# Retention attention and a squared-ReLU FFN on one core: attention visits of two chunks, another seven-product scheme, fixed rows of operations

## The chip, the cores and the metric

The kernel runs on one core of one Trainium2 chip. The metric is the device time of one execution in microseconds; the time shown is the median of several runs. The profiles are those of one execution each, and their span reaches from the first to the last instruction.

TensorE (PE in the profile) multiplies, VectorE (DVE), ScalarE (ACT) and GpSimd (POOL) do the elementwise work, and SyncE (SP) issues nearly all transfers. Each engine executes its own instructions in the order in which they were emitted and waits on semaphores for the others.

## The reference

```python
state = np.zeros((B, H, D, D), dtype=np.float32)
for t in range(S):
    state = gamma[None, :, None, None] * state + np.einsum('bhd,bhe->bhde', k[:, :, t], v[:, :, t])
    y[:, :, t] = scale * np.einsum('bhd,bhde->bhe', q[:, :, t], state)
...
x = np.ascontiguousarray(attn_out.transpose(0, 2, 1, 3)).reshape(B * S, H * D)
h = np.maximum(x @ w_in, 0.0)
return (h * h @ w_out).astype(np.float32)
```

There are 4 batches of 768 positions, 8 heads of 64; this gives 3072 tokens of 512 numbers. w_in is 512 x 2048, w_out 2048 x 512. All inputs and the output are float32; the kernel multiplies in bf16.

## The kernel before, in words

**Attention by chunks.** The tokens are cut into 24 chunks of 128 (six for each batch), each of two halves of 64. For a chunk, the kernel forms scores of keys against queries inside each half, masks them (P, into `pt`), and forms the sum of key times value of each half. These sums are added up to the running states (S, `state`). The output is values times masked scores plus the state applied to the queries (`apply`, first within the half's own row group, then `cross` after a drain of TensorE and a semaphore), scaled and written to `xt` by Y. The chunks 0 to 3 go in pairs in another layout (`together`, `pair_visits`). From chunk 4 on, `visit(m, n)` is one stretch on TensorE: values and states of chunk m, with scores and sums of chunk n between its two applies. The scores lie in one half of each bank of `sc`, the sums in the other; `yy` holds the outputs. All of these are 64 x 64 matmuls. The keys and queries must first be cast to bf16 (ck, cq) and transposed to `qkT`: on TensorE for the first chunks, from chunk 7 on by a DMA transpose on SP (X, line 761).

**FFN.** The chunks are grouped in 13 blocks of one or two. `ffn1` (F1) multiplies w_in by a block's `xt` in groups, one PSUM bank of 512 numbers each: eight matmuls of 128 x 256 for a block of two chunks, sixteen of 128 x 128 for a block of one. A bank is read by R (ReLU on ScalarE, into one of two buffers `r`) and squared into `h` by Q (ScalarE or VectorE). For the first four chunks `ffn2` (F2) multiplies plainly by w_out. For the others `products` does two chunks (a unit, named by its first chunk) by a scheme of seven products instead of eight: the 2 x 2 blocks are two chunks by two halves of the 2048 inner columns on one side, two halves of the inner rows by two halves of the output columns on the other. Five sums of blocks of `h` per unit (S1, S2, S5, S6, S7, line 1007), five sums of blocks of w_out (T1, T3, T4, T6, T7, in two halves each, made once, line 982), seven products M1 to M7 of eight matmuls each (line 1032), and reads that combine them: e4 and cc on ScalarE (128 x 256 and 128 x 512), t1, u1, w, c on VectorE (two of 128 x 256, two of 128 x 512; line 1050).

**Banks.** Four PSUM banks `fps` are shared by the F1 groups, F2, the products (a unit holds two, A and B, from their first product to the last read), and the transposes of the first chunks.

**The order.** All operations are recorded in a `Plan` with durations, dependencies and priorities. `schedule` places them one by one, each time the one that could start first by its model, ties by priority. Two tables steer it: `HOME` fixes the engine of some operations, `RANK` the priority of others. `dma_order` ranks the loads. The operations are then emitted in the order of their planned starts, and that order is what each engine executes. Around the first 65 us the loads of q, k, v and of the two weights (1 MB or 512 KB each) come through SP's queue in that order; each weight piece is cast to bf16 (cwin, cwout) on POOL, ScalarE or VectorE before it is used.

Of the kernel before, what the change touches and what calls it, by code (L numbers as in the profile page):

```python
# [18 lines left out]
class Plan:  # L19
# [14 lines left out]
    HOP = 0.15  # L34

# [5 lines left out]
    def add(self, name, eng, dur, reads=(), writes=(), fn=None, prio=0.0, lat=0.0, bank=None, after=(), count=0, slot=None, lock=()):  # L41
# [19 lines left out]
        if name in HOME:  # L61
            eng = {HOME[name]: eng[HOME[name]]}
        prio = RANK.get(name, prio)
        self.ops.append(dict(i=i, name=name, eng=eng, flex=flex, deps=sorted(deps), fn=fn,
                             prio=prio, lat=lat, bank=bank, count=count, slot=slot, lock=lock))
        return i

    def schedule(self, nbanks, max_open, nslots):
# [12 lines left out]
        for o in ops:  # L81
            for e in o["eng"]:
                eng_free.setdefault(e, 0.0)
                pool.setdefault(e, set())
                if left[o["i"]] == 0:
                    pool[e].add(o["i"])
# [15 lines left out]
        while done < n:  # L102
            best = None
            for eng, cand in pool.items():
                ef = eng_free[eng]
                for i in cand:
# [17 lines left out]
                    key = (t, o["prio"], i)  # L124
                    if best is None or key < best[0]:
                        best = (key, i, eng)
            assert best is not None, "no operation can be placed"
            (t, _, _), i, eng = best
            o = ops[i]
            for e in o["eng"]:  # L130
                pool[e].discard(i)
# [34 lines left out]
            else:  # L166
                if eng == "PE":
# [21 lines left out]
                    if any(before < x <= issued for x in range(self.BLOCK0 - self.AHEAD, issued + 1, self.BLOCK)):  # L189
# [14 lines left out]
                end[i] = t + dur + o["lat"]  # L204
# [15 lines left out]
            for u in users[i]:  # L220
                same = list(ops[u]["eng"]) == [eng] and not move
                ready_at[u] = max(ready_at[u], start[i] + dur if same else end[i] + self.HOP)
                left[u] -= 1
                if left[u] == 0:
                    for e in ops[u]["eng"]:
                        pool[e].add(u)
# [11 lines left out]
AHEAD = 4  # L238
WARM = 20.0
FILL = 0.215  # L240
WARMING = 18.4
PACE = 8
LEAD = 2
# [5 lines left out]
CVT = {'DVE': 0.69, 'POOL': 1.07}  # L249
TCAST = {'DVE': 0.43, 'ACT': 0.63, 'POOL': 0.64}  # L250
TEVAC = {'ACT': 0.6, 'DVE': 0.62}
NPAIR = 2
F2LAG = 3.5
F2WAIT = 4
LAST = [256, 128, 128]
CAST = {"k": {"DVE": 0.43, "ACT": 0.63, "POOL": 0.64}, "q": {"DVE": 0.43, "ACT": 0.63, "POOL": 0.64}}
WCAST = {"DVE": 0.43, "ACT": 0.63, "POOL": 0.64}
EVAC = {"ACT": 0.6, "DVE": 0.62}
WPRIO = {"in": -2.0, "out": 2.0, "sum": 3.0}
# [3 lines left out]
SQUARE = {"DVE": 0.7, "ACT": 0.63}  # L263
WSUM = {"DVE": 0.69}
ASUM = {"DVE": 0.69}
LAGS = {
# [941 lines left out]
```

## Time and profile before

| | |
|---|---|
| time, median of 3 runs | 203.87 us (203.72 to 205.05) |
| span of the profiled execution | 202.7 us (its own time is not listed; the median is 1.2 us longer than this span) |
| granted TensorE clock | 1.000 |
| busy: TensorE, its weight loads, VectorE, ScalarE, GpSimd | 192.8, 159.4, 150.0, 130.3, 31.3 us |
| F1 groups (L936): 832 matmuls | 94.0 us |
| products (L1032): 560 matmuls | 70.1 us (39.4 + 20.3 + 10.4) |
| plain F2 (L1108): 64 matmuls | 15.0 us |
| transfers | 38.46 MB, mean 190 GB/s |

How to read it: a matmul's time runs from its start to its modelled end, and matmuls overlap, so a mean of 264 ns for one does not mean that one comes every 264 ns; the steps in the chain do (eight in 0.87 us). The elementwise engines overlap too: neighbours on VectorE start 0.60 us apart where each is shown with 0.68. "Idle before" with an arrow names what ended the wait.

### The profile page before, as it was taken

The numbers are of one execution on the slowest core, as the hardware profiler recorded it, in microseconds if no ns is written. First come the engines' busy times: TensorE is split into PE (matmuls) and PEld (weight loads), VectorE is DVE, ScalarE is ACT, GpSimd is POOL, SyncE is SP. The second block draws the span as 40 slices with busy tenths as digits, with TensorE's granted clock in tenths as the row PEclk, the third lists the DMA queues.
The fourth block names the chain that finished last, engine by engine and source line by source line (L and its number), as shares of the span: only waits on it lengthen the run. The fifth ranks groups of instructions, "written<-read, shape, count | busy, mean of one in ns | idle before, by whom it ended". The sixth has DMA issues, their size and how long they took to land.

```text
span 202.7 us, 7020 instructions
## 1 busy us (share of the span) xinstructions
PE 192.8 (95%) x3032; PEld 159.4 (79%) x3032; DVE 150.0 (74%) x283; ACT 130.3 (64%) x229; POOL 31.3 (15%) x56
## 2 busy tenths in 40 slices
PE   8886999899989999999999999999999999999992
PEld 6554887664577888888888888888888888888881
DVE  3486449569849988969898888878998784934762
ACT  8565888788871883787975485569375873835210
POOL 6541252220102101310211012203010000000000
PEclk9999999999999999999999999999999999999999
DMA  5999999999999999999999999999676100111313
GB/s 159 290 314 320 348 344 330 361 246 210 236 191 219 231 247 212 205 234 186 148 240 165 261 211 218 178 222 194 143 145 97 48 17 3 52 52 55 102 55 105
DMA packets 97935, 38.46 MB, mean 190 GB/s; under 512 B 81008, under 2 KB 94320, under 8 KB 97904
## 3 DMA queue, kind: packets, MB, share of 16 engines
q1 hardware_dynamic: 97760, 37.89, 86.2%
q8 instruction: 23, 0.38, 0.8%
q10 hardware_dynamic: 144, 0.13, 0.2%
q14 instruction: 8, 0.07, 0.1%
HBM read 27.26 MB, written 6.29 MB: 166 GB/s over the span
## 4 chain that ended last, share of the span: by engine, by line
PE 75%; DMA 15%; SPq 5%; POOL 1%; DVE 1%; issue 1%; ACT 0%; DVEq 0%
PE fps L936 33%; PE fps L1032 29%; DMA kn<-in_k_dram 8%; PE fps L1108 6%; DMA wst<-in_moe_w_in_dram 4%; DMA qkT<-kqs 3%; SPq L910 3%; PE yy L787 2%; SPq L537 2%; PE yy L802 1%; PE sc L813 1%; PE sc L824 1%; POOL w_in L522 1%; DVE wu L1050 1%; POOL h L522 0%
## 5 line engine op out<-in xcount | busy, mean ns | idle before, releaser
L936 PE MATMUL fps<-xt,w_in 128*128 128x256 bf16 (+1 forms) x832 | 94.0, 264 | 1.6 <-ACT w_in L518 1.2
L936 PEld LDWEIGHTS <-w_in 128*128 128x128 bf16 x832 | 74.8, 98 | 11.5 <-ACT w_in L518 2.0
L943 ACT ACTIVATE r<-fps 128x512 f32<-128x512 f32 x96 | 56.4, 592 | 34.6 <-PE fps L936 28.6
L950 ACT ACTIVATE h<-r 128x512 bf16<-128x512 f32 x63 | 39.1, 627 | 1.4
L1032 PE MATMUL fps<-wst,h 128*128 128x256 bf16 x320 | 39.4, 273 | 0.0
L1032 PEld LDWEIGHTS <-h 128*128 128x128 bf16 x320 | 31.0, 98 | 3.9
L952 DVE TENSOR_TENSOR h<-r 128x512 bf16<-128x512 f32 x33 | 22.8, 705 | 8.7 <-ACT r L943 8.6
L1032 PEld LDWEIGHTS <-wst 128*128 128x128 bf16 x240 | 23.3, 98 | 2.8
L1007 DVE TENSOR_TENSOR wst<-h 128x1024 bf16<-128x1024 bf16 x30 | 19.4, 685 | 2.9 <-ACT h L950 2.6
L1032 PE MATMUL fps<-w_out,wst 128*128 128x256 bf16 x160 | 20.3, 273 | 0.0
L728 DVE TENSOR_TENSOR vs<-vn,vf 128x512 bf16<-128x512 f32 x20 | 13.8, 691 | 6.3 <-DMA vn<-in_v_dram 6.3
L889 DVE TENSOR_TENSOR xt<-yy,yf 128x512 bf16<-128x512 f32 x20 | 13.7, 687 | 3.5 <-PE yy L802 3.4
L522 POOL CAST kqs<-kn 128x512 bf16<-128x512 f32 x12 | 8.0, 666 | 51.0 <-DMA kn<-in_k_dram 32.3
L1108 PE MATMUL fps<-w_out,h 128*128 128x512 bf16 x64 | 15.0, 379 | 0.7 <-DVE w_out L520 0.7
L1007 DVE TENSOR_TENSOR h<-h 128x1024 bf16<-128x1024 bf16 x20 | 14.0, 729 | 0.2
L880 DVE TENSOR_TENSOR state<-sc,state 128x256 bf16<-128x256 f32 x33 | 13.8, 418 | 0.5
L867 DVE TENSOR_TENSOR pt<-sc,cmask 128x512 bf16<-128x512 f32 x20 | 13.6, 681 | 0.0
L522 POOL CAST kqs<-qn 128x512 bf16<-128x512 f32 x11 | 6.9, 626 | 42.9 <-DMA qn<-in_q_dram 30.6
L1050 DVE TENSOR_TENSOR wu<-fps,wu 128x512 f32<-128x512 f32 (+1 forms) x16 | 9.1, 572 | 5.0 <-ACT osb L1060 2.8
L1108 PEld LDWEIGHTS <-h 128*128 128x128 bf16 x64 | 5.9, 98 | 6.8 <-issue 0.8
L1060 ACT ACTIVATE osb<-fps 128x512 f32<-128x512 f32 x10 | 5.9, 594 | 8.3 <-PE fps L1032 8.3
L1050 DVE TENSOR_TENSOR osb<-fps,osb 128x512 f32<-128x512 f32 (+1 forms) x15 | 9.0, 601 | 2.6 <-PE fps L1032 1.7
(85 smaller groups left out, 173.4 us busy)
## 6 DMA issues: line engine op xcount, KB each, us to landing
qn<-in_q_dram SPq DMA_DIRECT2D x20, 256.0 KB, 5.1
kn<-in_k_dram SPq DMA_DIRECT2D x20, 256.0 KB, 5.6
vn<-in_v_dram SPq DMA_DIRECT2D x20, 256.0 KB, 5.2
out_dram<-osb SPq DMA_DIRECT2D x19, 256.0 KB, 3.3
wst<-in_moe_w_out_dram SPq DMA_DIRECT2D x4, 1024.0 KB, 10.1
wst<-in_moe_w_in_dram SPq DMA_DIRECT2D x4, 512.0 KB, 8.4
wst<-in_moe_w_in_dram SPq DMA_DIRECT2D x2, 1024.0 KB, 8.3
kn<-in_k_dram SPq DMA_DIRECT2D x2, 512.0 KB, 4.3
```

The source lines that it names most:

```text
L522: nc.gpsimd.tensor_copy(o, t)
L728: lambda: nc.vector.tensor_tensor(out=o[:], in0=t.rearrange("s (h d) -> s h d", h=H), in1=vf[:, i, :, None].to_broadcast([P, H, D]), op=AL ...
L880: f = lambda cc=cc, j1=j1, j0=j0: nc.vector.tensor_tensor(out=sts[j1][:], in0=cc, in1=sts[j0][:], op=ALU.add)
L889: lambda: nc.vector.tensor_tensor(out=xt[:, :, u * C : u * C + C].rearrange("s p (g t) -> s g p t", g=2), in0=yy[:, :, 0:256].rearrange("s ...
L936: nc.tensor.matmul(ps[:, u * n : u * n + n], lhsT=w_in_bf[j][:, cb, c * P : (c + 1) * P], rhs=xt[:, cb, cols], start=(cb == 0), stop=(cb = ...
L943: nc.scalar.activation(o, t, AF.Relu)
L950: nc.scalar.activation(hv, rv, AF.Square)
L952: (nc.vector if on == "DVE" else nc.gpsimd).tensor_tensor(out=hv, in0=rv, in1=rv, op=ALU.mult)
L1007: lambda on, o=a[name], x=a[x], y=a[y], op=op: (nc.vector if on == "DVE" else nc.gpsimd).tensor_tensor(out=o, in0=x, in1=y, op=op), prio=c ...
L1032: nc.tensor.matmul(ps[:, 256 * half : 256 * half + 256], lhsT=a[left][:, f], rhs=right(f), start=(first and f == 0), stop=True, skip_group ...
L1050: return lambda ps: nc.vector.tensor_tensor(out=o, in0=ps[:, lo:hi], in1=y, op=op)
L1108: nc.tensor.matmul(ps[:, 0:w], lhsT=h2[:, fb, u * C : u * C + C], rhs=w_out_bf[j][:, c, ns], start=(fb == 0), stop=(fb == NFB - 1))
```

## The change

**Visits of two chunks.** From chunk 10 on, `visit2(ms, ns)` does two chunks of outputs and two chunks of scores and sums in one stretch. The scores of both chunks fill `sc`, the outputs of both fill `yy`. The sums no longer fit there: they go to two `fps` banks, one for each half of the chunks, which are opened ahead of the stretch (U, an entry of the plan without instructions, and V) and closed by the state additions. The visit of 9 with 10 and 11 comes first, then 10-11 with 12-13 and so on, at the end 22-23 alone. Chunks from 10 on are loaded and prepared in pairs.

**The seven products.** Four sums of blocks of `h` per unit (H1 to H4) and four of w_out blocks (T1 to T4), again seven products. The reads of a unit are: e (ScalarE, 128 x 512), u (VectorE), v (an addition in SBUF, on POOL in six units and on VectorE in four), ca (ScalarE), cb, cd and cc (VectorE), all of 128 x 256. The two reads ca and cb take one half each of the same bank. Each output row of 128 x 512 is stored by one transfer.

**Fixed rows.** `HOME`, `RANK`, the priorities and `dma_order` go. The table `TURNS` lists for every engine all its operations in order, and `schedule` only takes the next of a row; it still works out times, and the emitted order is that of the planned starts. The planned durations are shorter (0.602 for 0.69 of VectorE, with a tail of 0.08 counted apart), which in fixed rows decides only how the rows are interleaved, and how many filling matmuls are put in at the start (35 for 36). Among the rows: the first FFN group is F1.0.4 instead of F1.0.0, and its two casts are on POOL and ScalarE instead of both on ScalarE; the four F1 groups of chunk 4 (F1.2) stand ahead of the first plain F2 group; the stores st0 and st1 stand behind the first DMA transpose X7 instead of before it. VectorE has 290 operations for 269, ScalarE 213 for 229, POOL 39 for 47; SP has 117 in both.

```diff
@@ -82,8 +81,20 @@
...
+        turns = {e: [known[x] for x in TURNS[e].split()] for e in pool}
...
+        def offer():
+            for e, x in turns.items():
+                if at[e] < len(x) and left[x[at[e]]] == 0:
+                    pool[e].add(x[at[e]])
...
@@ -236,117 +244,104 @@
...
-PAIRS_A = {"S1": ((0, 0), (1, 1), ALU.add, None), "S5": ((0, 0), (0, 1), ALU.add, None),
-           "S2": ((1, 0), (1, 1), ALU.add, None), "S6": ((1, 0), (0, 0), ALU.subtract, (1, 0)),
-           "S7": ((0, 1), (1, 1), ALU.subtract, (0, 1))}
...
+PAIRS_B = {"T1": ((0, 1), (0, 0)), "T2": ((1, 1), "T1"), "T3": ((1, 1), (0, 1)), "T4": ((1, 0), "T2")}
+PAIRS_A = {"H1": ((1, 0), (1, 1), ALU.add, None), "H2": ("H1", (0, 0), ALU.subtract, None),
+           "H3": ((0, 0), (1, 0), ALU.subtract, (1, 0)), "H4": ((0, 1), "H2", ALU.subtract, None)}
...
+TURNS = {
...
+    "PE": (
...
+        "F1.1.12 V4. F1.1.14 F1.0.12 F1.2.8 F1.2.0 F1.2.4 F1.2.12 F2.2.0 F2.0.0 F2.0.1 F2.2.1 Tk5 F2.2.2 F2.0.2 "
+        "Tq5 F2.0.3 F2.2.3 F2.3.0 V.5 F2.3.1 F2.1.0 F2.1.1 V5.6 F2.1.2 F2.3.2 F1.3.0 F1.3.8 V6.7 F1.3.12 F2.3.3 "
+        "F2.1.3 V7.8 F1.3.4 M1.4 F1.4.4 F1.4.6 F1.4.10 M5.4 F1.4.8 F1.4.0 F1.4.14 M2.4 F1.4.2 F1.4.12 M6.4 V8.9 "
...
@@ -879,19 +850,84 @@
...
+    def visit2(ms, ns):
...
+        def fn():
+            for x, m in enumerate(ms):
+                values(m, x)
+                apply(m, 0, x)
+            if ms:
+                nc.tensor.drain(fusable=True).then_inc(turn, 1)
+                turns[0] += 1
+            for x, n in enumerate(ns):
+                scores(n, x)
+            for x, n in enumerate(ns):
+                sums(n, [fps[o1[sub]["bank_index"]][:, 256 * x : 256 * x + 256] for sub in range(2)], x == 0)
+            if ms:
+                nc.tensor.wait_ge(turn, turns[0])
+                for x, m in enumerate(ms):
+                    apply(m, 1, x)
...
@@ -1005,19 +1043,19 @@
...
+            1: ((0, 0), lambda f: wb(0, 0, f), bkey(0)),
+            2: ((0, 1), lambda f: wb(1, 0, f), bkey(1)),
+            3: ("H4", lambda f: wb(1, 1, f), bkey(1)),
             4: ((1, 1), lambda f: tb("T4", f), tkey("T4")),
...
+            5: ("H1", lambda f: tb("T1", f), tkey("T1")),
+            6: ("H2", lambda f: tb("T2", f), tkey("T2")),
+            7: ("H3", lambda f: tb("T3", f), tkey("T3")),
...
@@ -1031,59 +1069,52 @@
...
+        product(1, "A", 0, "open")
+        product(5, "A", 1, "use")
+        read("e", "ACT", 0.48, "A", (), ke, lambda ps: nc.scalar.activation(e, ps[:], AF.Copy))
+        product(6, "B", 0, "open")
+        read("u", "DVE", 0.341, "B", ke[:1], k0[1:], plus(o0[:, hi], lo, e[:, lo]))
...
+        product(2, "A", 0, "use")
+        product(3, "A", 1, "use")
+        pl.add(f"ca.{c0}", "ACT", 0.28, [f"gS{c0}A"], k0[:1],
+               lambda: nc.scalar.activation(o0[:, lo], fps[opened["A"]["op"]["bank_index"]][:, lo], AF.Copy), bank=("close", ("s", c0, "A"), 2))
+        pl.add(f"cb.{c0}", "DVE", 0.341, [f"gS{c0}A"] + k0[1:], k0[1:],
+               lambda: plus(o0[:, hi], hi, o0[:, hi])(fps[opened["A"]["op"]["bank_index"]]), bank=("close", ("s", c0, "A"), 2))
+        product(7, "B", 0, "use")
+        read("cd", "DVE", 0.341, "B", k1[1:], k1[1:], plus(o1[:, hi], lo, o1[:, hi]))
+        product(4, "B", 0, "use")
+        read("cc", "DVE", 0.341, "B", ke[:1], k1[:1], plus(o1[:, lo], lo, e[:, lo]), close=True)
...
```

414 lines of the change are left out of this document (204 added, 210 removed), and 107 rows, old and new, of tables (HOME, RANK, TURNS).

## The prediction

> **What bounds the kernel now.** I read the busy line first, then the chain that ended last, then TensorE's timeline around a visit, around the early waits and at the end. The busy line and the slices:
>
> ```profile
> PE 192.8 (95%) x3032; PEld 159.4 (79%) x3032; DVE 150.0 (74%) x283; ACT 130.3 (64%) x229; POOL 31.3 (15%) x56
> PE   8886999899989999999999999999999999999992
> PE 75%; DMA 15%; SPq 5%; POOL 1%; DVE 1%; issue 1%; ACT 0%; DVEq 0%
> ```
>
> TensorE is the bound; in stretches of 5 us it is busy throughout from 65 us to 195 us (0.08 us idle in all). What can shorten the kernel is thus less TensorE time per piece of work, or fewer of its early waits. First a visit (the chain's columns are start, us, what):
>
> ```profile
> 88.49 0.87 PE fps L1032 x8
> 89.36 0.25 PE yy L787 x16
> 89.61 0.07 PE yy L802 x8
> 89.68 0.13 PE sc L813 x16
> 89.80 0.14 PE sc L824 x16
> 89.94 0.09 PE yy L802 x8
> 90.03 0.98 PE fps L936 x8
> 91.01 0.87 PE fps L1032 x8
> ```
>
> An FFN group of eight 128x256 matmuls takes 0.87; the one behind the visit takes 0.98. So this visit costs 0.67 + 0.11 = 0.78 us. The starts in the timeline say what of it is work: values 89.30 to 89.44 (0.14), first apply to 89.50 (0.06), scores to 89.63 (0.13), sums to 89.76 (0.13), and a second apply like the first (0.06): 0.52. The other 0.26 is paid once per visit: 0.11 on entering (0.25 for work of 0.14), some 0.03 at the wait before the second apply, 0.11 on leaving. The waits put 4.2 us over 19 visits on the weight loads of L787 as "issue", the same entrance.
>
> Then the early waits and the end (timeline rows):
>
> ```profile
> 17.54 1.35 PE L936 MATMUL fps<-xt,w_in 128*128 128x256 bf16 x8 [1.03 <-ACT w_in L518]
> 19.05 1.05 PE L936 MATMUL fps<-xt,w_in 128*128 128x256 bf16 x8 [0.16 <-ACT w_in L518]
> 39.05 1.02 PE L1108 MATMUL fps<-w_out,h 128*128 128x512 bf16 x4 [0.68 <-DVE w_out L520]
> 58.39 0.32 PE L813 MATMUL sc<-qkT 64*64 64x64 bf16 x16 [0.53 <-DMA qkT<-kqs]
> ...
> 197.03 1.91 PE L1032 MATMUL fps<-wst,h 128*128 128x256 bf16 x16
> ...
> 197.86 1.55 DVE L1050 TENSOR_TENSOR wu<-fps,wu 128x512 f32<-128x512 f32 x3 [1.95 <-ACT osb L1060]
> 199.11 0.69 ACTq L1077 DMA_DIRECT2D out_dram<-wu  x1
> 199.44 0.34 SPq L1077 DMA_DIRECT2D out_dram<-wu  x1
> ```
>
> The first two wait for casts of w_in, the third for a cast of w_out, the fourth for the DMA transpose of chunk 7. After the last product (to 198.94) come 3.8 us of addition, store and landing.
>
> The span is 202.7 us, the median 203.87. The profiled execution's own time is not listed, so I sum against the span and carry the 1.2 us between them. Within 1% (2.0 us) a measurement of this kernel can hardly tell from no change.
>
> **Double visits: -1.8 us.** Before, 15 visits run from chunk 9/10 to the end; after, 8 (9 with 10-11; six of two and two; 22-23 alone). The matmuls are the same, so 7 entrances and exits go: 7 x 0.26 = 1.8. Bounds: if only the entrance (0.11) is per visit and the rest grows with the work, 7 x 0.11 = 0.8; if the 0.03 and the drain vanish too, 2.0. The added wait on TensorE (second applies behind the drained first ones) has two chunks' scores and sums, 0.52, before it, twice today's cover; at 22-23, without scores, it stays open as it is for 23 now (166.75 to 167.40). Queued behind it is one FFN group.
>
> **The seven-product scheme: 0 on TensorE.** Both have seven products of eight matmuls per unit. On VectorE each unit has four operand sums for five (10 x 0.69 = 6.9 us less), eight weight sums for ten (1.4 less), and four reads of 128x256 at 0.42 for two of these and two of 128x512 at 0.69 (10 x 0.54 = 5.4 less). The built rows give VectorE more as well: 39 squares for 33 (6 x 0.70 = 4.2), 20 weight casts for 5 (15 x 0.41 = 6.2), 12 casts of q and k for 4 (3.3), four of the ten new SBUF additions (1.7): in sum it stays near 150. ScalarE loses six squares, seven weight casts and three others, some 10 us of 130. Neither is the bound: an instruction shown with 0.68 starts 0.60 after its neighbour (60.01, 60.61, 61.21), so VectorE is emptier than 74%. POOL's six new additions of 128x256 have no row; between 0.42 (VectorE, that shape) and 1.04 (POOL's 128x512 with two operands) I take 0.6; POOL is busy 15%, so 0.
>
> One read changes more than its size. The bank of products 2 and 3 is read half by ScalarE (ca) and half by VectorE (cb). In the order of the built program each cb waits for ScalarE, so a VectorE queue with cb at its head stands up to 0.38 + a hand-over. The same hand-over is in the tail above: ScalarE's read ends at 197.83, VectorE starts at 197.86. Behind cb stand Q, H and S operations, for which TensorE's banks and groups wait. Ten times 0.4 is 4 us of VectorE, if nothing else stood there; with TensorE some groups ahead I take 0.1 of it on the path, bounds 0 and 4. [...]
>
> **The rows up to 65 us: -0.6 us.** TensorE's lost time there is 0.5 (the first FFN group takes 1.35 for 0.87, its two casts follow each other on ScalarE), 0.16, 0.68, 0.53, and 0.25 at the visit of chunks 7 and 8 (start 62.42, scores 62.87 where 62.62 would do): 2.1. After, the first group's casts stand on POOL and ScalarE, and the four F1 groups of chunk 4 (16 x 57 ns = 0.91 each) come ahead of the first F2 group, so the w_out cast has 3.6 us more: both waits go, -1.3. But the next limit is late already: the transposes of chunks 7 and 8, issued at 52.24 and 55.79, land at about 58.3 and 62.83. On SP they are moved past: two output stores stand behind instead of before the first (0.73 each at 50.62), and v9 instead of k9 before the second. That brings the second issue at most 1.4 earlier, to 54.4; casts of k8 and q8 end at 54.70 now, so hardly more. From issue to landing takes 4.5 to 7.0, median 6.0 in this stretch. With 6.0 it lands at 60.4, 2.4 earlier. The new row has 0.91 + 0.87 = 1.8 less work ahead of that visit, which remains to be done: net -0.6. Bounds: landing as now, +1.8; in time for everything, -2.1.
>
> **The steady part: +0.2.** A double visit takes two of the four FFN banks for its sums (before, they lay in the free half of the visit's own bank), until VectorE has made up to four state additions; F1 groups then turn in the remaining banks. After visit 12-13/14-15 VectorE's row is S, S, S, Y, Y, Q, S: 4 x 0.34 + 3 x 0.60 = 3.2 us to the second bank, 1.1 to the first. An F1 group needs 0.87 plus a ScalarE read of 0.60 and hand-overs. I take +0.1 here and +0.1 for cb. Bounds 0 and +6 (below).
>
> **The end: 0.** After the last product there is one 0.42 addition and a store of 128x256 by ScalarE's queue, as now (199.11, 0.69 long, against 0.34 on SP); +-0.3.
>
> Sum: -1.8 - 0.6 + 0.2 = -2.2: span 200.5, time 201.7.
>
> **The rivals.**
> - *The transposes eat it* (within 1%). If the transpose of chunk 8 lands only as much earlier as it is issued earlier (1.4), the early part gives +0.4, and the sum is -1.2: 202.7; landing as now, 204.1. For it: its DMA took 7.04 and TensorE waits for both transposes now. Against: the stores moved behind.
> - *The banks stall* (slower). During the 3.2 us in which a visit holds two banks, an F1 group every 1.1 instead of 0.87 loses 0.2 to 0.3 on each of three groups; where products hold the other two banks and an F1 group is next, TensorE stands for the 1.1 to 2 us to the first release. At 0.9 for each of seven visits, 6.3, the time is 203.9 - 2.4 + 6.3 = 207.8. It turns slower than before from 0.34 per visit and slower by over 1% from 0.63. For it: four banks in all and ca ahead of cb. Against: product groups stand behind most visits, in banks they already hold, and VectorE has gaps.
> - *All early waits vanish* (faster): -1.8 - 2.1 + 0.2: 200.2.
> - *The fixed cost isn't one* (the change doesn't do what it says): 0.11 per visit; -0.8 - 0.6 + 0.2: 202.7.
>
> **Chances.** Faster by over 1%: 0.52, of which my sum 0.36 and the vanished waits 0.16. Within 1%: 0.34 (transposes 0.22, small fixed cost 0.12). Slower by over 1%: 0.14 (banks). The range of 8 in 10 runs from 199.7, the vanished waits with 2.0 for the visits and 0.3 at the end, to 204.2, the transposes landing as now.
>
> **What would show it.** Visits of two chunks at 1.3 us against 2 x 0.78; no wait for w_out at about 39 us; a wait for qkT at the visit of 7 and 8 of at most 1.2 us; TensorE idle under 0.5 us from 65 us on; cb starting at the end of ca. Wrong would be: groups of L936 that wait for ScalarE or VectorE behind the visits, or a longer first stage.

## The result, and the profile after

The changed kernel is **slower**: 213.12 us (211.09 to 213.73) beside 204.46 us (203.72 to 206.00) of the kernel before on the same chip, a ratio of 1.038 with a 95% interval of 1.030 to 1.046. The forecast was 201.7 us, faster.

The page of the changed kernel, in the lines that answer to those of before: busy time, TensorE's slices, the chain that ended last.

```profile
span 211.4 us, 7041 instructions
...
PE 191.4 (91%) x3027; PEld 160.1 (76%) x3031; DVE 151.1 (71%) x304; ACT 119.6 (57%) x213; POOL 27.7 (13%) x48
...
PE   2997999999779997989889979979999999999991
...
PE 51%; DMA 15%; SPq 13%; ACT 9%; issue 5%; DVE 4%; POOL 2%; POOLq 0%; ACTq 0%
```

TensorE's busy time fell by 1.4 us, but it is now spread over 8.7 us more: 91% instead of 95%. Between 53 and 143 us eight slices (5.3 us each) show 7 or 8, where the kernel before has a single 8 and otherwise nines. In the chain, TensorE's own share fell from 75% to 51%, and SyncE's queue rose from 5% to 13%. VectorE has not become the bound (151.1 us for 150.0).

TensorE's timeline of the changed kernel, only rows in which it waited, from 17 us on and for 0.2 us or more (start, us, what, in brackets the idle time and what ended it):

```profile
18.03 0.54 PE L586 MATMUL yy<-qkT 64*64 64x128 bf16 x16 [1.48 <-issue]
...
53.99 0.32 PE L760 MATMUL yy<-pt,vs 64*64 64x64 bf16 x16 [1.34 <-DVE pt L839]
...
63.03 0.32 PE L786 MATMUL sc<-qkT 64*64 64x64 bf16 x16 [1.01 <-DMA qkT<-kqs]
...
77.11 1.03 PE L1070 MATMUL fps<-wst,h 128*128 128x256 bf16 x8 [0.44 <-DVE osb L1093]
82.34 0.44 PE L786 MATMUL sc<-qkT 64*64 64x64 bf16 x32 [1.27 <-DMA qkT<-kqs]
92.72 1.03 PE L971 MATMUL fps<-xt,w_in 128*128 128x256 bf16 x8 [0.79 <-ACT r L978]
102.03 1.05 PE L1070 MATMUL fps<-wst,h 128*128 128x256 bf16 x8 [0.79 <-DVE pt L905]
107.87 0.32 PE L786 MATMUL sc<-qkT 64*64 64x64 bf16 x16 [0.67 <-DMA qkT<-kqs]
122.77 0.45 PE L786 MATMUL sc<-qkT 64*64 64x64 bf16 x32 [1.37 <-DMA qkT<-kqs]
134.37 1.03 PE L1070 MATMUL fps<-wst,h 128*128 128x256 bf16 x8 [0.20 <-DVE wu L1093]
139.50 1.05 PE L1070 MATMUL fps<-wst,wst 128*128 128x256 bf16 x8 [1.15 <-ACT h L985]
```

The wait for w_out at 39 us is gone in this profile, as forecast. Behind 63 us, where the kernel before had nothing but stretches without a gap, there are eight waits: 0.44 + 1.27 + 0.79 + 0.79 + 0.67 + 1.37 + 0.20 + 1.15 = 6.7 us. Each costs a little more than is shown, because the modelled end of a group overlaps the next one when there is no wait (a group is shown with 1.04 and the next starts 0.87 later): 0.17 each, 1.4 in all, so 8.0 (6.68 + 1.36).

**Where the 8.7 us of span came from.** The scores of chunk 8 start at 62.87 before and 63.03 after, with 1.8 us less work done ahead of them (the prediction's 0.91 + 0.87): 1.9 us lost by then. From there to the last product 8.0 of waits, less the seven visits saved, 1.8. The last product ends at 198.94 before and at 206.99 after (205.95 + 1.04); from there to the end it is 3.8 before and 4.4 after: 0.6. Sum: 1.9 + 8.0 - 1.8 + 0.6 = 8.7.

The end of the changed kernel, in the timeline of all engines:

```profile
205.95 1.04 PE L1070 MATMUL fps<-wst,h 128*128 128x256 bf16 x8
206.20 0.38 ACT L1104 ACTIVATE osb<-fps 128x256 f32<-128x256 f32 x1 [3.82 <-PE fps L1070]
206.62 0.42 DVE L1093 TENSOR_TENSOR osb<-fps,osb 128x256 f32<-128x256 f32 x1 [0.86 <-ACT osb L1104]
...
207.49 1.51 ACTq L1115 DMA_DIRECT2D out_dram<-wu  x1
```

cb starts at 206.62, just behind ca's 206.20 + 0.38, so the hand-over that the prediction read out of the order is there. The last store takes 1.51 us to issue on ScalarE's queue, where it took 0.69 before. This is not a fixed price of the new end: in two of the kernels below, with the same last operations, it took 0.37 us.

A double visit, in the chain of the changed kernel (start, us, what):

```profile
157.53 0.87 PE fps L1070 x8
158.40 0.25 PE yy L760 x16
158.65 0.06 PE yy L775 x8
158.72 0.13 PE yy L760 x16
158.84 0.07 PE yy L775 x8
158.91 0.27 PE sc L786 x32
159.18 0.23 PE fps L798 x21
...
159.58 0.98 PE fps L971 x8
```

From 158.40 to 159.58 and 0.11 in the group behind it: 1.29 us, against 2 x 0.78 for two single visits (two others without a wait come to 1.27 and 1.38). So TensorE does get what the prediction counted; what is lost is lost in waits.

### The profile page after: what moved, and what is told of

It reads as the page before. It is cut to its first block, busy times and chain, and to the rows that moved or that the text cites. A ratio compares the mean times of both kernels' runs of the same rounds, so it can differ in the third digit from the quotient of the medians.

```text
span 211.4 us, 7041 instructions
## 1 busy us (share of the span) xinstructions
PE 191.4 (91%) x3027; PEld 160.1 (76%) x3031; DVE 151.1 (71%) x304; ACT 119.6 (57%) x213; POOL 27.7 (13%) x48
## 4 chain that ended last, share of the span: by engine, by line
PE 51%; DMA 15%; SPq 13%; ACT 9%; issue 5%; DVE 4%; POOL 2%; POOLq 0%; ACTq 0%
PE fps L971 21%; PE fps L1070 21%; DMA qkT<-kqs 10%; SPq L694 8%; ACT r L978 5%; SPq L736 3%; DMA vn<-in_v_dram 3%; ACT h L985 3%; PE fps L1211 2%; DMA qn<-in_q_dram 2%; DVE h L987 1%; PE sc L786 1%; PE fps L602 1%; PE yy L775 1%; PE fps L556 1%
## 5 line engine op out<-in xcount | busy, mean ns | idle before, releaser
L971 PEld LDWEIGHTS <-w_in 128*128 128x128 bf16 x832 | 75.7, 98 | 10.1 <-issue 1.0
L985 ACT ACTIVATE h<-r 128x512 bf16<-128x512 f32 x57 | 35.2, 628 | 1.2
L987 DVE TENSOR_TENSOR h<-r 128x512 bf16<-128x512 f32 x39 | 27.8, 721 | 9.2 <-ACT r L978 8.7
L1070 PE MATMUL fps<-wst,h 128*128 128x256 bf16 x160 | 20.7, 273 | 1.4 <-DVE pt L905 0.8
L1070 PE MATMUL fps<-wst,wst 128*128 128x256 bf16 x160 | 20.8, 273 | 1.1 <-ACT h L985 1.1
L1070 PE MATMUL fps<-w_out,h 128*128 128x256 bf16 x160 | 20.8, 273 | 0.0
L919 DVE TENSOR_TENSOR state<-fps,state 128x256 bf16<-128x256 f32 x23 | 9.6, 419 | 4.1 <-PE yy L775 3.4
L1096 ACT ACTIVATE wst<-fps 128x512 f32<-128x512 f32 x10 | 6.0, 595 | 11.2 <-PE fps L1070 11.2
L1093 DVE TENSOR_TENSOR osb<-fps,osb 128x256 f32<-128x256 f32 x15 | 6.3, 420 | 6.7 <-ACT osb L1104 5.6
L1093 DVE TENSOR_TENSOR osb<-fps,wst 128x256 f32<-128x256 f32 x15 | 6.3, 421 | 5.9 <-PE fps L1070 4.8
L1070 PE MATMUL fps<-w_out,wst 128*128 128x256 bf16 x80 | 10.4, 273 | 0.0
```

Source lines behind the costliest of these rows:

```text
L919: nc.vector.tensor_tensor(out=sts[j1][:], in0=cc, in1=sts[j0][:], op=ALU.add)
L971: nc.tensor.matmul(ps[:, u * n : u * n + n], lhsT=w_in_bf[j][:, cb, c * P : (c + 1) * P], rhs=xt[:, cb, cols], start=(cb == 0), stop=(cb = ...
L985: nc.scalar.activation(hv, rv, AF.Square)
L987: (nc.vector if on == "DVE" else nc.gpsimd).tensor_tensor(out=hv, in0=rv, in1=rv, op=ALU.mult)
L1070: nc.tensor.matmul(ps[:, 256 * half : 256 * half + 256], lhsT=a[left][:, f], rhs=right(f), start=(first and f == 0), stop=True, skip_group ...
L1093: return lambda ps: nc.vector.tensor_tensor(out=o, in0=ps[:, x], in1=y, op=ALU.add)
```

## The experiments

Four explanations stood against each other after the result: the **transposes** arrive late (3.3 of the 6.7 us shown are waits for qkT); a double visit holds two **banks** and gives VectorE a long turn; the new **scheme**; and the **order** of the fixed rows itself.

### The parts one by one, in the rows of before

The changed file without double visits, and with rows taken from the order of the kernel before, into which only the new scheme's operations were put:

```diff
-DOUBLE = 10
+DOUBLE = 99
...
 TURNS = {
     "POOL": (
-        "iota2 iota3 iota cmask cmask2 ident cq2.0 cq2.1 ck2.0 cv2.0 cv2.1 cwin2.0 cwin3.0 ck4 cwout1.1 cwout2.3 "
+        "iota3 ident iota iota2 cmask2 cmask ck0.0 cq0.1 cv0.0 cv0.1 ck2.1 cv2.0 cwin1.2 cwin2.0 cq4 cwin3.0 "
...
```

> The new seven-product scheme alone: single visits as before, and every engine's row in the order that the kernel before emitted, with the new sums, products and reads put at the places of the old ones. Theory A (the fixed rows of the change cost the time, scheme and double visits don't): 203 to 205.5 us, TensorE without waits of over 0.3 us from 65 us on. Rival B (the scheme costs: cb stands behind ca, its hand-overs reach TensorE): 207 us or more, with waits of L1070 or L971 for VectorE or ScalarE in the steady part.

Measured: 210.13 us, ratio 1.027 (1.024 to 1.031). A row of VectorE's timeline of this kernel:

```profile
71.23 0.42 DVE L1094 TENSOR_TENSOR osb<-fps,wst 128x256 f32<-128x256 f32 x1 [4.61 <-DMA out_dram<-osb]
```

The scheme's first addition into an output buffer (u) comes earlier in a unit than the old scheme's, and waits 4.61 us for the store of the buffer's earlier content; TensorE then stands for 2.02 us at 72.31. So the scheme, which the prediction found neutral by its durations, is not neutral in rows that were made for another: the reuse of a buffer moved.

Then the same rows with the double visits in the place of the first of the two single ones, and the second chunk's loads, conversions and transpose moved ahead:

```diff
-DOUBLE = 99
+DOUBLE = 10
...
     "POOL": (
...
-        ck10 v.6 cq12 ck13 cq13 cq14 ck15 v.8 cq15 ck16 ck17 v.10 cq18
+        ck10 v.6 cq12 ck13 cq13 cq14 ck15 cq15 v.8 ck16 ck17 cq19 v.10 cq18
...
```

> As the run with the scheme alone, and double visits from chunk 10 on, each at the place of the first of the two single visits; the loads, casts and transposes of the second chunk of a pair moved ahead in the rows. Theory A (rows): 1 to 2 us under the run with the scheme alone, since seven visits' fixed 0.26 us go. Rival C (a pair needs its second transpose about one visit earlier than the transfers can bring it): waits of L786 for qkT of 0.5 to 2 us at three or more of the seven visits, and 2 to 6 us over the run with the scheme alone.

Measured: 220.25 us, 1.077 (1.073 to 1.080). TensorE has no waits for transposes to speak of (0.2 us), but 5.4 us for sums of h on VectorE, and a sum of 3.3 for first-layer groups and products that wait for the visit's outputs and state additions. Both kernels tell only that rows can't be reused for changed operations; they don't settle the price of a part.

### Two single repairs of the changed kernel

The identity, for which TensorE waits 3.10 us at the start, second on GpSimd instead of last of its constants:

```diff
-        "iota2 iota3 iota cmask cmask2 ident cq2.0 cq2.1 ck2.0 cv2.0 cv2.1 cwin2.0 cwin3.0 ck4 cwout1.1 cwout2.3 "
+        "iota3 ident iota iota2 cmask2 cmask cq2.0 cq2.1 ck2.0 cv2.0 cv2.1 cwin2.0 cwin3.0 ck4 cwout1.1 cwout2.3 "
```

> The changed kernel with GpSimd's row begun as before (ident second instead of sixth), all else alike. Theory D (the late ident costs at the start: TensorE's filling matmuls begin 3 us later, its clock is 0.82 to 0.84 from 15 to 25 us, and the first F1 group is 1.5 us late): the dip goes, first F1 group at 17.0 to 17.8 us, time 1 to 2.5 us lower. Rival E (the transposes that come later set the time anyway): the first stage is as much earlier and the waits for qkT at chunks 7/8 and behind are as much longer; time within 0.7 us of the changed kernel.

Measured: 212.51 us, 1.037 (1.030 to 1.043), no difference. The wait went, but the first FFN group started at 19.29 instead of 18.93. In this profile TensorE then waited 1.74 us up to 9.76, and its granted clock was 0.50 from 10.1 to 20.4 us (see the last section), so the run does not tell what the late identity costs by itself. The scores of chunk 8 started at 62.27, without a wait, instead of 63.03.

Six buffers for the transposed queries and keys instead of five:

```diff
-    NLD, NBF, NQT, NXT, NH2, NWS, NOSB, NST = 4, 5, 5, 3, 3, 4, 3, 6
+    NLD, NBF, NQT, NXT, NH2, NWS, NOSB, NST = 4, 5, 6, 3, 3, 4, 3, 6
```

> The changed kernel with six buffers qkT instead of five, so that the transpose of a pair's second chunk needn't wait for the end of the visit before. Theory C1 (the buffer makes the double visits' transposes late): the waits of L786 for qkT at 107.9 (0.67) and 122.8 (1.37) go or halve, time 1 to 2 us lower. Rival C2 (SP's row and the loads ahead of the transposes make them late): the waits stay within 0.3 us of what they were, time within 0.7 us.

Measured: 214.39 us, 1.044 (1.036 to 1.052), no gain, and the same four waits for qkT: 1.01, 0.52, 0.74 and 1.04, where the changed kernel has 1.01, 1.27, 0.67 and 1.37. Two became shorter, by 1.1 us together, and the time did not fall. So the number of these buffers alone does not hold the transposes; what SyncE's row has ahead of them stays.

### Two by two: each part with and without the other, ordered by one rule

To compare the parts without hand-made rows, four kernels were ordered by the priorities of before (its tables, with the change's planned durations; a visit of two has the priority of its second chunk): neither part, the scheme alone, the visits alone, both.

```diff
-TURNS = {
...
+                    key = (t, o["prio"], i)
...
-DOUBLE = 10
+DOUBLE = 99
```

(the last two lines only in the kernels with single visits)

> Neither part of the change: single visits and the old scheme, but with the planned durations of the change and the order taken by priorities again (no fixed rows). It is the base of the next three. Theory A (the fixed rows cost the time): within 1.5% of the kernel before, 203 to 207 us. Rival F (the shorter planned durations alone make orders that don't hold on the chip): 208 us or more.

> The new scheme with single visits, ordered by priorities. Theory A: within 1 us of the base with neither part. Rival B (the scheme itself costs, by cb behind ca or by writes into output buffers that wait for stores): 2 us or more over that base, with VectorE waiting at L1093's line for ScalarE or for out_dram transfers.

> Double visits with the old scheme, ordered by priorities. Theory A: 1 to 2 us under the base with neither part (seven visits' fixed 0.26 us). Rival C (the second chunk's transpose comes late, whatever the order): waits for qkT of 0.5 us or more at three or more of the eight visits, and a time 2 us or more over that base.

> Both parts, ordered by priorities: the changed kernel without its fixed rows. Theory A (rows): 4 us or more under the changed kernel's 211 to 213.7, at 203 to 207 us. Rival G (double visits and scheme cost, the rows don't): within 2 us of the changed kernel.

| ordered by the rule | old scheme | new scheme |
|---|---|---|
| single visits | 212.10 us, 1.035 (1.026 to 1.044) | 211.19, 1.031 (1.025 to 1.037) |
| visits of two | 215.60, 1.055 (1.046 to 1.064) | 214.63, 1.047 (1.041 to 1.054) |

The **scheme** moves the time by -0.9 and -1.0, which is within the intervals: no difference that can be measured, where 0 was forecast. The **visits** cost 3.5 and 3.4 us, where the forecast had -1.8. And with neither part the rule with the changed planned durations is already 7.5 us above the kernel before; what of this is due to the durations and what to the tables was not taken apart. The fixed rows (213.12) are 1.5 better than the rule with both parts, which is within the intervals.

TensorE's largest waits from 60 us on, first of the kernel with single visits (what waited, what ended it, us in total, times, longest), then of the one with visits of two, both with the old scheme:

```profile
PE fps L1053 <- ACT r L1060: 1.9, 1, 1.9
PE fps L1053 <- DVE wu L1168: 1.9, 1, 1.9
PE sc L868 <- DMA qkT<-kqs: 1.1, 2, 1.0
```

```profile
PE fps L1053 <- DVE state L1001: 5.7, 3, 3.5
PE sc L868 <- DMA qkT<-kqs: 2.2, 2, 1.2
```

Here, with visits of two, the first-layer groups wait 5.7 us for state additions, which give back the banks that the visit holds: the rival of the prediction, as named there. Whether that is also the loss of the changed kernel, the next runs ask.

### What holds the changed kernel: transposes, visits, or the order of additions

Without the fourteen transposes of chunks 10 to 23 (three of the seventeen stay):

```diff
-                   lambda: nc.sync.dma_start_transpose(out=qkT.rearrange("p x j t -> p (x j) t"),
-                                                       in_=t.rearrange("s x j a d -> s (x j a d)")))
+                   (lambda: nc.sync.dma_start_transpose(out=qkT.rearrange("p x j t -> p (x j) t"),
+                                                       in_=t.rearrange("s x j a d -> s (x j a d)"))) if m < 10 else (lambda: None))
```

> The changed kernel with the twelve transposes of chunks 10 to 23 on SyncE's queue left out of the timed work (all but those of chunks 7, 8 and 9); the visits read whatever stands in the buffers, so from chunk 10 on queries and keys are stale numbers and only the time is used. Theory A (transposes): the waits of TensorE for qkT from 65 us on, 0.67 + 1.27 + 1.37 us, vanish and nothing takes their place: 3.3 us and 0.16 us each for the modelled ends make 3.8, so 213.1 falls to about 209.3; the wait for chunk 8 at 63 us stays. Theory B (VectorE's long turn behind a visit of two chunks, and the two banks that it holds): the waits move to VectorE's tiles, and 211.5 to 213 is left.

Measured: **207.41 us**, 1.011 (1.005 to 1.017), 5.7 us less than with them. TensorE's waits from 62 us on in this kernel:

```profile
PE sc L786 <- DMA qkT<-kqs: 1.1, 1, 1.1
PE fps L1070 <- DVE kqs L512: 1.0, 1, 1.0
PE fps L1070 <- DVE osb L1093: 0.5, 1, 0.5
PE fps L971 <- DVE state L919: 0.2, 1, 0.2
```

The one wait for qkT that is left is chunk 8's, whose transpose stays. Nothing took the place of the others: behind chunk 8's, 1.7 us of waits are left of 6.7. So theory A holds, and more was saved than the 3.8 us that it counted, because the waits for ScalarE's r at 92.72 and for its h at 139.50 went too. Leaving the transposes out also frees SyncE's queue of the 1.3 to 4.0 us that each takes to issue; the run does not tell what of the 5.7 us is late landing and what is this.

The same left out of the kernel before, to see whether transposes are dear as such:

> The kernel before with the transposes of chunks 10 to 23 left out, as in the changed kernel's run without them (stale queries and keys from chunk 10 on; only the time is used). If the transposes are dear in the changed kernel alone: the kernel before showed 0.1 us of waits for them from 63 us on, so 203.5 to 204.7 here against 204.5 to 205, and the 5.7 us that the changed kernel saved without them is a price of the change. If their traffic is dear everywhere (other loads come earlier without it): 200 to 202.

Measured: 204.53 us, 1.000 (0.998 to 1.003). In the kernel before, the transposes cost nothing that can be measured (0.5 us to either side). The 5.7 us (by the ratios: 0.027 of 205 us, 5.5, with an interval of some 2 us to either side) are a price of the change.

Each visit of two undone into two single ones, in the changed kernel's own rows:

```diff
-DOUBLE = 10
+DOUBLE = 99
...
     "PE": (
...
-        U12-13.14-15 V12-13.14-15 F1.6.14 F1.6.0 F1.6.10 F1.6.12 F1.7.10
+        V13.14 F1.6.14 F1.6.0 F1.6.10 F1.6.12 V14.15 F1.7.10
...
     "DVE": (
...
-        S14.0 S14.1 S15.0 Y13 Y12 Q6.0 S15.1 Q6.10 P14 P15
+        P14 S14.0 S14.1 Y13 Q6.0 P15 Q6.10 S15.0 S15.1 Y14
...
```

> The changed kernel with its own fixed rows, but each visit of two chunks undone into two single visits: the first in the place of the double one, the second four TensorE operations later, and VectorE's masks, sums and outputs in the order of the single visits at the same places. Scheme and all other rows are as in the change. The prediction's reckoning (a visit has 0.26 us of fixed cost): 7 more visits cost 1.8, so 214.9. Theory B (the double visit's long turn on VectorE and its two banks cost 3.4 to 3.5, as in the two pairs ordered by a rule): 209.5 to 211, though the places of the second visits were not tuned and may cost 1 us. Theory C (the fixed rows are as dear with either kind of visit): within 1 of 213.1.

Measured: 212.80 us, 1.040 (1.031 to 1.049): theory C. The rows are as dear with single visits; the seven more visits, 1.8 us, are less than these intervals (some 1.9 us each) can show. TensorE's waits of this kernel from 62 us on:

```profile
PE sc L786 <- DMA qkT<-kqs: 4.4, 4, 1.7
PE fps L1070 <- DVE osb L1093: 2.8, 4, 1.2
```

The sum of waits for transposes is the same (4.4 us, and 4.3 in the changed kernel, 1.0 of each for chunk 8), so most of the lateness is not due to the merging as such. By chunks it differs: 10 and 16 are still waited for (0.97 and 0.79), 15 no longer, and 20 is new (1.66). The row of SyncE shows a reason for these three: X11 stands ahead of X10, X17 ahead of X16 and X21 ahead of X20, so the pair's first chunk comes last.

VectorE's row with each double visit's state additions ahead of its masks and outputs:

```diff
-        S18.0 S18.1 P19 S19.0 u.12 Y17 Y16 cb.12 P18 ck23 S19.1
+        S18.0 S18.1 S19.0 S19.1 P19 u.12 Y17 Y16 cb.12 P18 ck23
```

> The changed kernel with one edit in VectorE's row: behind each visit of two chunks its state additions come first, ahead of masks and outputs, so that the two banks are given back some 1.5 to 2.5 us earlier; masks and outputs come up to 1.4 us later. Theory bank (waits of first-layer groups for the two banks): 1.5 to 2 us of the 0.79 + 0.79 + 0.44 us of bank waits go, about 211.3. Theory VectorE's turn (its length counts, not its order): the time stays within 1 of 213.1, and waits appear at the second-layer products or at the next visit's values instead.

Measured: 213.30 us, 1.040 (1.032 to 1.048), no difference, with waits at the same places (0.68 us for ScalarE's r at 92.69) and of 6.2 us in all behind 65 us, for 6.7. The order in which the two banks come back is not what costs time in the changed kernel, as far as these intervals (some 1.6 us each) can show.

The same idea in the kernel ordered by the rule (additions first in priority):

```diff
+    m = _re.fullmatch(r"S(\d+)\.\d", name)
+    if m and int(m[1]) >= DOUBLE:
+        return -500 + int(m[1])
```

> The kernel ordered by priorities with visits of two chunks and the scheme of before, where first-layer groups waited 5.7 us for banks held by the visit's state additions; here these additions have the first turn on VectorE as soon as their visit is done. Theory bank: the waits for state fall under 1.5 us and the time from 215.6 to 211.5 to 212.5, as with single visits. Theory VectorE's turn: the waits come back at other tiles (masks, outputs, squares) and 214 to 216 is left.

Measured: 216.36 us, 1.055 (1.044 to 1.066), no difference, and still 4.2 us of waits for state. VectorE's timeline in the longest of them, which ended at 99.89:

```profile
93.53 1.90 DVE L1125 TENSOR_TENSOR wst<-h 128x1024 bf16<-128x1024 bf16 x3
95.35 1.70 DVE L1125 TENSOR_TENSOR h<-h 128x1024 bf16<-128x1024 bf16 x2
...
97.57 0.41 DVE L1002 CAST state<-fps 128x256 bf16<-128x256 f32 x1
```

The visit's products were done at about 94.3, but the first of its additions runs at 97.57, behind the five sums of a product unit, which stand ahead of it in the emitted row. As the additions had the first priority, the visit must have come later by the plan. A priority does not help where the row was fixed from planned times and the real times differ. So this run did not test what it was meant to.

### Moving the transposes, and the additions, by hand

Six buffers, and SyncE's row in the order of the chunks with each pair's transposes ahead of the later loads (and on ScalarE the conversions of the queries of chunks 15 and 17 exchanged):

```diff
     "SP": (
...
-        st4.0 st4.1 ldk14 X12 ldq17 X13 ldq15 ldk17 X14 ldq16 ldv15 X15 ldk16 ldq18 ldq19 ldv16 ldk18 ldk19 ldv17 X17 ldq20 st6.1 X16
+        ldk14 X12 X13 st4.0 st4.1 ldq15 X14 X15 ldq17 ldk17 ldq16 ldv15 ldk16 ldv16 ldv17 X16 X17 ldq18 ldk18 ldq19 ldk19 ldq20 st6.1
...
```

> The changed kernel with six buffers for the transposed queries and keys instead of five, and SyncE's row from chunk 9 on in the order of the chunks, each pair's two transposes ahead of the loads and stores of later chunks; on ScalarE the conversion of chunk 15's queries changes places with that of chunk 17's. Nothing is left out. If the transposes are late because the row and the five buffers hold them: of the 5.7 us that they cost, 2 to 4 come back, 209 to 211. If what holds them is the conversions on the other engines' rows and the pair's earlier need: within 1 of 213.1, with the waits for qkT still there.

Measured: 219.58 us, 1.074 (1.065 to 1.083): 6.5 us worse, though all waits for qkT behind chunk 8 are gone. The rows of TensorE, ScalarE and VectorE around 105 us in this kernel:

```profile
107.33 1.78 PE L972 MATMUL fps<-xt,w_in 128*128 128x256 bf16 x8 [3.76 <-DVE osb L1094]
```

```profile
105.47 0.63 ACT L511 ACTIVATE kqs<-qn 128x512 bf16<-128x512 f32 x1 [5.97 <-DMA qn<-in_q_dram]
```

```profile
106.51 0.43 DVE L513 CAST kqs<-kn 128x512 bf16<-128x512 f32 x1 [3.44 <-DMA kn<-in_k_dram]
```

The loads of chunk 17 now stand behind the transposes of 14 and 15, which went out from 95.24 to 100.27 us; ahead of its transposes SyncE stands from 108.48 to 113.05 us, 4.4 us of it for a conversion on ScalarE. The conversions of chunk 17 stand in ScalarE's and VectorE's rows ahead of the reads of FFN banks, so these engines wait for the loads, the banks are not given back, and TensorE stands for 3.76 us. So in these fixed rows a transpose that goes out earlier pushes a load, a load a conversion, and a conversion a bank.

The same with two edits to the early rows (chunk 5's mask and one of its state additions ahead of conversions that wait for loads, and one first-layer group ahead of the visit at 63 us):

```diff
     "DVE": (
...
-        cq7 ck7 WT4.0 cv6 S5.0 P5 ck8
+        cq7 S5.0 P5 ck7 WT4.0 cv6 ck8
...
     "PE": (
...
-        V7.8 F1.3.4 M1.4
+        F1.3.4 V7.8 M1.4
...
```

> The changed kernel with the six buffers and SyncE's row of the run before it, and two edits to the early rows: on VectorE the mask of chunk 5 and one state addition go ahead of a conversion and a values product that wait for loads, and on TensorE one first-layer group goes ahead of the visit that waited 1.01 us for the transpose of chunk 8. If the early waits (1.34 and 1.01 us) were lost time: 1 to 2 below the run with the transposes early alone. If the transpose of chunk 8 sets the pace there: the same as that run, within 0.6.

Measured: 220.84 us, 1.080 (1.074 to 1.085), no better. The scores of chunk 8 still waited 0.97 us for the transpose (1.07 in the run before it), and started at 64.46 instead of 63.61. So the waits at 54 and 63 us are not lost time that could be had by itself; the transpose of chunk 8 sets the pace there.

The state additions moved in the finished order itself, in the kernel ordered by the rule: each directly behind its visit, and the sums of h that stood shortly ahead of them behind them (the second step is not shown):

```diff
+    for i in sequence:
+        if i not in late:
+            order.append(i)
+            if pl.ops[i]["name"][0] == "V" and pl.ops[i]["count"] >= 65:
+                to = pl.ops[i]["name"].split(".")[1].split("-")
+                order += [held[f"S{x}.{sub}"] for x in to for sub in range(2) if held.get(f"S{x}.{sub}") in late]
...
```

> The kernel ordered by priorities with visits of two chunks and the scheme of before (215.6), in which VectorE did up to five sums of a product unit (3.3 us) between a visit and the rest of its state additions; here, in VectorE's row itself, the visit's additions stand ahead of those sums and next to each other. Theory bank: the 5.7 us of first-layer waits for state fall under 1.5 and the time to 211 to 213. Theory VectorE's turn: the waits reappear elsewhere and 214 to 216 is left.

Measured: 242.56 us, 1.18 (1.17 to 1.19). The waits for state are gone, but some 25 us of others came: 18.2 for VectorE's reads of product banks (osb and wu), 4.9 for outputs (xt), 2.0 for a sum of h. Why the reads came late was not taken apart. The run tells nothing of the banks.

### Banks alone: visits of two and single ones without their key-value products

In both kinds of kernel the key-value products are left out from chunk 10 on, so that a visit opens no bank; the additions stay on VectorE, on a constant tile.

```diff
-                sums(n, [fps[o1[sub]["bank_index"]][:, 256 * x : 256 * x + 256] for sub in range(2)], x == 0)
...
-                    cc = fps[o1[sub]["bank_index"]][:, 256 * x : 256 * x + 256].rearrange("s (p t) -> s p t", p=NJ)
+                    cc = yf[:, :, 0:64]
```

> The kernel ordered by priorities with visits of two chunks and the scheme of before (215.6), from chunk 10 on without the key-value products (32 small products per chunk on TensorE left out, the visit opens no bank); VectorE's state additions stay, on a constant tile instead of a bank. Compared with the next kernel, which leaves out the same with single visits. Theory bank: without banks to hold, the visits of two chunks come out 1 to 2 faster than the single ones (7 fewer visits of 0.26 us make 1.8), where with the products they were 3.5 slower. Theory VectorE's turn or the transposes: they stay 2 to 4 slower.

> The kernel ordered by priorities with single visits and the scheme of before (212.1), from chunk 10 on without the key-value products, and VectorE's state additions on a constant tile, as in the run before it. The products were 14 chunks of 32 at about 0.3 us a chunk, so 4.2 less than 212.1 if TensorE sets the time: about 208. The difference to the run before it decides: -1 to -2 for theory bank, +2 to +4 for the others.

Measured: visits of two 209.97 us, 1.027 (1.021 to 1.032); single visits 209.64 us, 1.027 (1.021 to 1.033). The 3.5 us between the two kinds (some 2.6 to either side) became 0.3 (some 1.7 to either side). That lies between the two theories, of which one asked for -1 to -2 and the other for +2 to +4. So in the kernels ordered by the rule most of the price of a double visit goes with the key-value products and the banks that they hold, within wide intervals, but the forecast gain of 1.8 does not appear either. TensorE's largest waits of the kernel with visits of two, from 62 us on:

```profile
PE fps L1045 <- DVE xt L1001: 3.8, 2, 3.6
PE sc L868 <- DMA qkT<-kqs: 2.8, 3, 1.1
```

First-layer groups now wait for the visit's outputs (xt), and transposes are waited for 2.8 us, against 1.1 in the kernel with single visits and without the products.

## Why the prediction was wrong, point by point

- **The visits, -1.8.** The size of the saved work was right: 1.29 us for a double visit where the prediction had 1.3. But this is a saving of TensorE's work, and it shows as time only while nothing else is late. In the rule's kernels it turned into +3.5, without the banks into +0.3; in the changed kernel's rows undoing it changed nothing that can be measured.
- **The scheme, 0.** Not contradicted: -0.9 and -1.0 in two pairs, within their intervals.
- **The rows up to 65 us, -0.6.** Wrong by 2.5: +1.9. The term that failed is the landing of chunk 8's transpose. The prediction took its issue from 55.79 to 54.4 and its landing to 60.4, because a load and two stores stood elsewhere on SP. It was issued at 56.13 and landed at about 63.0, 6.9 later. SyncE's row shows why it was not issued earlier:

```profile
50.93 1.07 SPq L694 DMA_DIRECT2D vn<-in_v_dram  x1
52.12 2.03 SPq L736 DMA_TRANSPOSE qkT<-kqs  x1
...
54.88 0.62 SPq L1151 DMA_DIRECT2D out_dram<-osb  x1
...
56.13 3.11 SPq L736 DMA_TRANSPOSE qkT<-kqs  x1
```

  The two stores are gone from the place ahead of chunk 7's transpose, but a load of v stands there instead, so this transpose went out at 52.12 for 52.24; and one of the two stores now stands between it and chunk 8's. In the chain that ended last the whole stretch from 39.05 to 56.13 is SyncE's queue, and then this transpose. "Landing as now, +1.8" was the true case. The w_out wait went as forecast, but that bought nothing, because chunk 8 could not come earlier.
- **The steady part, +0.2.** This is the step that failed most: 8.0 instead of 0.2. It counted the two banks and cb, and left out the transposes, whose rows the prediction had read only up to chunk 8. These cost 5.5 us, to within some 2 us (3.3 of it shown as waits for qkT, the rest in other waits that went with them). The kernel before issued one transpose at a time and, for chunks 10 to 15, 6.4 to 7.4 us ahead of its scores. The first of the next two fences has SyncE's transposes of chunks 14 and 15 before, the second those of after.

```profile
93.37 2.19 SPq L761 DMA_TRANSPOSE qkT<-kqs  x1
99.12 2.75 SPq L761 DMA_TRANSPOSE qkT<-kqs  x1
```

```profile
96.45 1.85 SPq L736 DMA_TRANSPOSE qkT<-kqs  x1
...
99.85 3.90 SPq L736 DMA_TRANSPOSE qkT<-kqs  x1
```

  Before, the scores that need them start at 100.72 and 105.86, one visit apart. After, both chunks are needed in one visit, whose scores started at 106.9 with chunk 14; chunk 15's transpose, issued at 99.85, was there at 107.87, 8.0 us later. For chunks 10 and 16, which were issued at 75.78 and 117.33, TensorE was ready at 81.1 and 121.4: leads of 5.3 and 4.1 us, where the median from issue to landing was 5.4 (4.8 before) and the longest 8.0 (7.0 before). So the lead had become shorter for chunks 10 and 16, and the landing longer for chunk 15, and either was enough to make TensorE wait.
- **The banks** (the rival that ended on the other side, 207.8). Its sign was right, and the mechanism exists: 5.7 us of waits for state additions in the rule's kernel, and 3.5 us that shrink to 0.3 without the banks. In the changed kernel itself no run shows it as a cause: the fixed rows put product groups directly behind four of the seven visits, bringing the additions forward changed nothing, and undoing the visits changed nothing. So that this rival had the right sign was luck as far as this kernel goes.
- **The transposes eat it** (the rival within 1%). The right mechanism with too narrow a bound: it was worked out for chunk 8 alone and limited to "landing as now".
- **The end, 0 within 0.3.** +0.6 in this profile, with 1.51 us instead of 0.69 for the issue of the last store on ScalarE's queue. With an issue of 0.37 us, in the run with single visits in the changed kernel's rows, the end took 3.5 us (209.62 to 213.1), 0.3 less than before. So the term itself was not wrong by a fixed amount.
- **cb behind ca.** The wait is there: VectorE waited 5.6 us for ca's reads, in six waits. No run here priced it on TensorE.

What stays open: 2 to 3 us of the loss remain without the transposes of chunks 10 to 23 (207.41 against 204.53). In that run's trace they lie in the early part: the scores of chunk 8 start at 63.93, 1.1 us later than before, with 1.8 less work done ahead of them, that is 2.8 (1.9 in the profile of the change). Behind that the waits that are left (2.2 with their modelled ends) and the 1.8 saved by the visits nearly cancel. No repair of the early rows brought the early loss back. And why the rule with neither part is 7.5 us above the kernel before was not taken apart.

## What to carry to other kernels

A saving of work on the bounding engine counts only if everything that feeds this engine keeps its lead: for each merged step, write down when its last input was issued, how long such a transfer took at worst, and when the step now needs it, over the whole run and not only where waits are visible before. Merging two steps brings the second one's inputs forward by a whole step, and the first one's release back by as much; but undo the merge once before blaming it, since here the wait for one chunk went with it and those for two others stayed. Where every engine runs a fixed row, a transfer, the conversion behind it and the bank read behind that form one chain, so that moving one of them alone (here the transposes, 6.5 us worse) can cost more than the wait that it removes.

## What the runs showed of the hardware

**Three pauses of TensorE, of 1.48, 1.74 and 3.76 us, were followed by a granted clock of 0.50 for 3.4, 10.3 and 3.4 us.** The stretches of 1 us of the changed kernel behind the wait at 18.03 (columns: stretch, length, the five engines' busy share, granted clock, DMA share, GB/s):

```profile
17.00:18.00 1.00, 0.00 (x0) 0.00 (x0) 0.65 (x2) 0.00 (x0) 0.00 (x0) 1.00 1.10 354
18.00:19.00 1.00, 0.97 (x33) 0.90 (x33) 0.39 (x1) 0.63 (x1) 0.00 (x0) 0.59 1.10 341
19.00:20.00 1.00, 1.00 (x6) 0.69 (x7) 1.00 (x3) 0.00 (x0) 0.00 (x0) 0.50 1.26 282
...
21.00:22.00 1.00, 0.93 (x44) 0.62 (x36) 0.12 (x1) 0.97 (x2) 0.58 (x1) 0.70 1.04 377
```

After 1.48 us without a matmul the clock of the changed kernel was 0.50 from 18.2 to 21.6 us, and the first FFN group took 1.89 us, where the kernel before shows 1.35. In the run with the transposes early, the pause of 3.76 us up to 107.33 was followed by 0.50 from 107.4 to 110.9, and the group behind it is shown with 1.78 instead of 1.03. With the identity moved ahead, a pause of 1.74 us up to 9.76 was followed by 0.50 from 10.1 to 20.4 us, during which TensorE was busy for 0.8 to 1.0 of every us. The length of a pause alone does not decide it in these runs: 1.03 us up to 17.54 in the kernel before and 3.10 us up to 4.51 in the changed kernel left the clock at 1.00. So did 2.23 us up to 54.82 in the run without transposes, as far as its mean clock of 0.997 tells (3.4 us at 0.50 in its span of 205.6 us would make 0.992). What else decides it was not shown. By an estimate from the two stretches of 3.4 us, such a wait costs up to 1.7 us on top of itself (half of 3.4, if TensorE has work for all of it and does it at half the pace). It is not what made chunk 8 late: the run without transposes kept 1.00 from 17 to 22 us, and its chunk 8 came at 63.93.
